# Attention and two feed-forward layers on one core: the order of attention's work from a greedy model in the kernel, and one ring of PSUM tiles for scores and maxima

## The chip, the cores and the metric

The kernel runs on one core of a Trainium2 chip. The metric is device time in microseconds (us), lower is better. Times are those of single executions, and the median of several runs stands for the kernel.

## The reference

Attention with a mask from hashing, over 2 batches of 8 heads (16 heads in all, 768 tokens, 64 dimensions), and then two feed-forward layers over 1536 tokens of 512 features (2048 inside). All data are fp32. Cut to what is computed:

```python
q_bits = (einsum('bhsd,dk->bhsk', q, proj) > 0)      # 6 bits, k_bits likewise
mask = q_bucket[:, :, :, None] == k_bucket[:, :, None, :]
scores = where(mask, scale * q @ k.T, -1e9)
scores = scores - max(scores, axis=-1)
attn = exp(scores)
attn = attn / (sum(attn, axis=-1) + 1e-09)
x = (attn @ v)  # heads side by side: (1536, 512)
h = x @ moe_w_in;   x = maximum(0.01 * h, h) @ moe_w_out
h = x @ moe2_w_in;  out = (h * cos(h)) @ moe2_w_out
```

## The kernel before, in words

Matmuls run in a reduced fp32 format (`F32R`), so each operand is split into a high part (a cast) and a low part (the value minus its cast), and a product takes three matmuls: high by high, high by low, low by high.

`attention` (L91) works head by head; each head has 768 = 6 x 128 keys, and 768 queries that are two halves of 384 columns (`HS`). Four buffers `AT` (L661) hold the split q and k of a head, its hash bits, and the row of the maxima. Per head n:

- `load_qk` (L125) loads the raw q and k, `prep_hi` (L143) casts them on VectorE and copies parts of the cast to other partitions by DMA, `prep_lo` (L149) subtracts on GpSimd, with one more copy by DMA.
- `bits_mm` and `bits_wr` (L197, L206), once per half: three matmuls with the hash directions, a comparison on VectorE, and two more copies by DMA after the second half. A differing bit lowers a score by a huge amount, and so masks it.
- `max_mm` and `max_red` (L218, L224), 12 of each: approximate scores of 128 queries by 384 keys in a one-bank PSUM tile `sm`, and their maximum on VectorE. `max_fin` (L231) joins the two halves, takes the maximum with a floor (for a query without any partner) and writes a 0/1 flag, in two small VectorE instructions on SBUF tiles. `max_row` (L238) turns both into rows by one matmul, ScalarE copies them out of PSUM, and DMAs put the maxima into `AT` and the flag into `E`, a tile of 2 rows.
- per 128 keys k: `qk` (L253, four matmuls into a two-bank tile `st`), `exp_a` and `exp_b` (L262, L273), `p_lo` (L282), `pv` (L296, four matmuls for part 0, two for part 1, into `pv`). A letter per k in `MODE` and `MODES` says how the exponential is split: A takes it twice on ScalarE, once rounded and once in place in PSUM, and subtracts on VectorE; B takes it once into `pf`, casts on ScalarE and subtracts on GpSimd; C casts on VectorE and subtracts on GpSimd; D casts and subtracts on VectorE.
- `pv_e` (L290) starts the accumulation with the sum of all v for queries that have no partner. `evac` (L310) copies the result and the sum of the exponentials out of PSUM. `recip` (L318) adds 1e-9, inverts, and spreads the inverse over 64 partitions by way of DRAM. `xmul`, `xhi`, `xlo` (L330 to L345) scale the result and split it into `XH` and `XL`, the input of the feed-forward layers.
- once in four heads: `load_v`, `v_hi`, `v_lo`, and `sum_v` with `sum_vr`, the sums of v over the tokens.

PSUM has eight banks: two `st` tiles of two banks, two `sm` tiles of one bank (maxima, bits, rows, sums), one `pv` tile of two. Each engine runs its instructions in the order in which the program issues them, and so does SyncE (SP) with its DMAs. The order is by sorted positions: `at` (L427) gives each step a number, head times 6 plus an offset from the table `K` (L37), and L473 issues the steps in the order of these numbers. Head 0 has its own code (`first`, `first_rest`, `max_whole`).

During heads 12 to 15 the first four chunks of feed-forward weights are prepared (`CHUNK_START`, `STAGE`, `Weights.stages` L490): they arrive as raw 64-bit words, and per chunk take two ScalarE, four VectorE and one GpSimd instruction of 128x1024. They use the memory of V and of the `AT` buffers as these come free. Then `moe` (L552) runs the two layers; it and the weights' code are the same before and after.

Of the kernel before, what the change touches and what calls it, by code (L numbers as in the profile page):

```python
# [30 lines left out]
MODE = "DBABBA"  # L31
MODES = {12: 'DBABBB', 13: 'BBABAA', 14: 'BBBBDA', 15: 'CDDDAA'}
ENG = dict(ph="V", pl="G", vh="G", vl="G", ev="A", xm="G", xh="V", xl="G")
CHUNK_START = (76.75, 83.91, 86.56, 96.03)
SHIFT = {2: 2.094}
STAGE = (0, 1.29, 1.88, 4.24, 4.46)
K = dict(  # L37
    ea=[0.01, 0.01, 0.01, 0.01, 0.01, 0.01],
    eb=[0.266, 0.025, 0.267, 0.02, 0.764, 0.862],
    lo=[0.733, 0.198, 0.93, 0.274, 0.938, 0.974],  # L40
    p0=[2.403, 2.19, 2.388, 2.41, 2.303, 1.7],
    p1=[2.578, 2.609, 2.72, 2.752, 2.806, 1.913],
    pe=2.084,
    ev=0.056,
    rec=10.899,
    xm=13.1,
    xh=16.761,
    xl=17.769,
    mx=[[0.364, 0.414], [0.085, 0.485], [0.328, 0.485], [0.328, 0.691], [0.237, 0.41], [0.523, 0.195]],
    rd=0.01,  # L50
    mf=-4.444,
    mr=-3.391,
    bm=[-12.668, -12.522],
    bw=0.01,
    ph=-15.546,
    pl=-15.374,
    ld=-24.393,
    vld=-30.087,
    vh=[-25.855, -12.685],
    vl=[-20.717, -11.738],  # L60
    sv=-2.83,
    svr=0.01,
    sv0=0.842,
    m1=[-5.464, -3.992, -1.927, -5.01, -3.499, -2.802],
    mf1=-1.615,
    mr1=-1.132,
)
GLV = 8
# [14 lines left out]
def f32(ap):  # L83
    return ap.bitcast(F32)
# [6 lines left out]
def attention(tc, XH, XL, AT, VH, VL, qkt, v, proj, cst, heads=NH, feed=()):  # L91
    nc = tc.nc
    T, V, A, G, Q = nc.tensor, nc.vector, nc.scalar, nc.gpsimd, nc.sync
    with ExitStack() as ctx:
# [39 lines left out]
        raw[0] = raw_p.tile([128, S], F32, name="raw")  # L134
        for h in range(2):
            Q.dma_start(raw[0][:, h * HS:(h + 1) * HS], qkt[0, 0][:, h * HS:(h + 1) * HS])
        Q.dma_start(cs, cst)
        thr, wgt = cs[64:BM, 128:129], cs[64:BM, 129:130]

        E = [con.tile([2, S], F32R, name=f"e{i}") for i in range(2)]  # L140
        SV = [con.tile([2, 4, 128], F32R, name=f"sv{i}") for i in range(2)]

        def prep_hi(n):  # L143
            at = AT[n % NR]
            copy(ENG["ph"], at[:, 0], raw[n])
            Q.dma_start(f32(at[0:64, 2]), f32(at[64:128, 0]))
            Q.dma_start(f32(at[0:64, 3]), f32(at[64:128, 0]))

        def prep_lo(n):  # L149
            at = AT[n % NR]  # L150
            eng(ENG["pl"]).tensor_tensor(at[:, 1], raw.pop(n), f32(at[:, 0]), op=ALU.subtract)
            Q.dma_start(f32(at[64:128, 3]), f32(at[64:128, 1]))

        vraw = {}

        def load_v(g):
            t = vraw_p.tile([128, C, 4, 64], F32, name="vraw")
            Q.dma_start(t, v[g // 2, :, :, (g % 2) * 4:(g % 2) * 4 + 4, :])
            vraw[g] = t

        def vsl(g, pr):
            return (t[g % 2][:, :, pr, 0:3:2, :] for t in (VH, VL))

        def v_hi(g, pr):
            copy(ENG["vh"], next(vsl(g, pr)), vraw[g][:, :, 2 * pr:2 * pr + 2, :])

        def v_lo(g, pr):
            hi, lo = vsl(g, pr)
            eng(ENG["vl"]).tensor_tensor(lo, vraw[g][:, :, 2 * pr:2 * pr + 2, :], f32(hi), op=ALU.subtract)

        svp = {}

        def sum_v(g):
            ps = sm_ps.tile([2, 2, 2, 64], F32, name="sm")
            vs = (VH[g % 2], VL[g % 2])
            for c in range(C):
                for j in range(2):
                    T.matmul(ps, ones2, vs[j][:, c, :, 0:3:2, :], start=(c == 0 and j == 0), stop=(c == C - 1 and j == 1))
            svp[g] = ps

        def sum_vr(g):
            ps = svp.pop(g)
            h2 = sv_p.tile([2, 4, 64], F32R, name="svh")
            l2 = sv_p.tile([2, 4, 64], F32, name="svl")
            psf = ps.rearrange("p a b d -> p (a b) d")
            V.tensor_copy(h2, psf)
            V.tensor_tensor(l2, psf, f32(h2), op=ALU.subtract)
            V.tensor_scalar(l2, l2, cs[0:2, 1:2], None, op0=ALU.mult)
            for par in range(2):
                dst = SV[g % 2].rearrange("p (a b) d -> p a b d", b=2)[:, :, par, par * 64:par * 64 + 64]  # L190
                src = h2.rearrange("p (a b) d -> p a b d", b=2)[:, :, par, :]
                sl = l2.rearrange("p (a b) d -> p a b d", b=2)[:, :, par, :]
                V.scalar_tensor_tensor(dst, f32(src), cs[0:2, 0:1], sl, op0=ALU.mult, op1=ALU.add)

        bps = {}

        def bits_mm(n, h):  # L197
            at = AT[n % NR]
            cols = slice(h * HS, (h + 1) * HS)
            ps = sm_ps.tile([128, HS], F32, name="sm")  # L200
            T.matmul(ps[0:BM], PB[0], at[:, 0, cols], start=True, stop=False)
            T.matmul(ps[0:BM], PB[1], at[:, 0, cols], start=False, stop=False)
            T.matmul(ps[0:BM], PB[0], at[:, 1, cols], start=False, stop=True)
            bps[n, h] = ps

        def bits_wr(n, h, spread=True):  # L206
            at = AT[n % NR]
            cols = slice(h * HS, (h + 1) * HS)
            V.tensor_scalar(at[64:BM, 0, cols], bps.pop((n, h))[64:BM], thr, wgt, op0=ALU.is_ge, op1=ALU.mult)
            if h == 1 and spread:  # L210
                Q.dma_start(f32(at[64:R76, 2]), f32(at[96:BM, 0]))
                Q.dma_start(f32(at[64:128, 1]), f32(at[0:64, 0]))

        mxt = {}

        mps = {}

        def max_mm(n, t, h):  # L218
            at = AT[n % NR]
            ps = sm_ps.tile([128, HS], F32, name="sm")  # L220
            T.matmul(ps, at[0:R76, 0, t * 128:(t + 1) * 128], at[0:R76, 2, h * HS:(h + 1) * HS], start=True, stop=True)  # L221
            mps[n, t, h] = ps

        def max_red(n, t, h):  # L224
            if (t, h) == (0, 0):
                mxt[n] = sm_p.tile([128, 2, C], F32, name="mx")
            V.reduce_max(mxt[n][:, h, t:t + 1], mps.pop((n, t, h)), axis=AX.X)  # L227

        met = {}

        def max_fin(n):  # L231
            mx = mxt.pop(n)
            me = sm_p.tile([128, 2, C], F32R, name="me")
            V.scalar_tensor_tensor(me[:, 0], mx[:, 0], -HALF_BIG, mx[:, 1 if n else 0], op0=ALU.max, op1=ALU.max)
            V.tensor_scalar(me[:, 1], f32(me[:, 0]), -HALF_BIG, None, op0=ALU.is_le)
            met[n] = me

        def max_row(n):  # L238
            me = met.pop(n)
# [8 lines left out]
        pt = {}

        def mode(n, k):  # L250
            return MODES.get(n, MODE)[k]

        def qk(n, k):  # L253
            at = AT[n % NR]
            ps = st_ps.tile([128, 2, 512], F32, name="st")
            for h in range(2):
                o = ps[:, h, 0:HS]
                T.matmul(o, at[0:R76 + 1, 2, k * 128:(k + 1) * 128], at[0:R76 + 1, 0, h * HS:(h + 1) * HS], start=True, stop=False)  # L258
                T.matmul(o, at[:, 3, k * 128:(k + 1) * 128], at[:, 1, h * HS:(h + 1) * HS], start=False, stop=True)  # L259
            pt[n, k] = [ps, None, None, None]  # L260
# [463 lines left out]
```

## Time and profile before

| | us |
|---|---|
| median of 3 runs | 836.24 |
| lowest, highest | 833.68, 840.98 |
| the profiled execution, its own time | 835.71 |
| its span, first to last instruction | 833.9 |
| TensorE busy in the span | 790.7 (95%) |
| VectorE busy | 554.1 (66%) |
| ScalarE busy | 404.7 (49%) |
| GpSimd busy | 421.1 (51%) |

Times in rows count from the start of the span. PE is TensorE, PEld its weight loads, DVE VectorE, ACT ScalarE, POOL GpSimd, SP SyncE. The last three numbers of a row of stretches are TensorE's granted clock (1.00 is 2.4 GHz), the DMA engines' busy share and GB/s. `L286` is line 286 of the kernel. The instruction that ends a wait is named behind an arrow. A matmul's row is longer than its share of TensorE, since matmuls overlap.

### The profile page before, as it was taken

How to read it: one execution, taken by the hardware profiler on the slowest of the kernel's cores; microseconds unless marked ns; L12 is line 12 of the kernel's file. 1: busy time of each engine (PE TensorE's matmuls, PEld its weight loads, DVE VectorE, ACT ScalarE, POOL GpSimd, SP SyncE). 2: the span in 40 equal slices, each digit the busy share in tenths (PEclk: the TensorE clock that was granted, in tenths of full speed). 3: DMA queues.
4: the chain of work that ended last, by engine and by line, in shares of the span. 5: the costliest groups of instructions: out<-in, count | busy, mean ns of one | idle time of the engine just before them, and what ended most of it. 6: DMA issues, size and time to landing. Idle time of an engine off the chain costs nothing. (4 is left out here: it accounts for less than half of the span.)

```text
span 833.9 us, 9909 instructions
## 1 busy us (share of the span) xinstructions
PE 790.7 (95%) x3648; PEld 669.9 (80%) x3648; DVE 554.1 (66%) x770; ACT 404.7 (49%) x592; POOL 421.1 (51%) x253
## 2 busy tenths in 40 slices
PE   5799899998997799999999999999899999999998
PEld 3688798898887777888888888888688888888886
DVE  6878888989988888654456536636736656753333
ACT  3355476565576454434234323454755645644442
POOL 4645578578677643336425515665623532542221
PEclk9999999999999899999999999999999999999999
DMA  4523434433351124212202202201211210000012
GB/s 127 156 59 89 110 89 98 120 97 88 79 172 61 39 99 196 101 66 105 83 0 102 101 1 101 101 1 57 95 51 51 101 51 0 1 1 1 0 51 101
DMA packets 24024, 62.60 MB, mean 75 GB/s; under 512 B 7636, under 2 KB 11380, under 8 KB 19880
## 3 DMA queue, kind: packets, MB, share of 16 engines
q1 hardware_dynamic: 23976, 61.97, 24.1%
q8 instruction: 29, 0.48, 0.2%
q14 instruction: 19, 0.16, 0.1%
HBM read 46.21 MB, written 3.19 MB: 59 GB/s over the span
## 5 line engine op out<-in xcount | busy, mean ns | idle before, releaser
L605 POOL TENSOR_TENSOR gl<-gf,gh 128x512 fp32r<-128x512 f32 x88 | 130.4, 1482 | 272.8 <-ACT gh L604 216.9
L618 PE MATMUL y<-gh,at 128*128 128x512 f32 x576 | 178.6, 391 | 1.9 <-ACT ys L624 1.8
L576 PE MATMUL h<-XH,at 128*128 128x512 f32 x576 | 142.8, 390 | 1.6 <-POOL XH L118 1.6
L618 PEld LDWEIGHTS y<-gh,at 128*128 128x128 f32 x576 | 108.4, 189 | 25.5 <-ACT ys L624 2.2
L576 PEld LDWEIGHTS h<-XH,at 128*128 128x128 f32 x576 | 108.3, 188 | 24.6 <-POOL XH L118 2.0
L618 PE MATMUL y<-gl,at 128*128 128x512 f32 x288 | 112.9, 392 | 0.7 <-POOL gl L605 0.7
L227 DVE TENSOR_REDUCE mx<-sm 128x1 f32<-128x384 f32 x180 | 95.7, 549 | 20.9 <-PE sm L221 19.2
L286 POOL TENSOR_TENSOR pl<-pf,ph 128x768 fp32r<-128x768 f32 x48 | 90.9, 1896 | 35.1 <-ACT ph L278 18.8
L585 DVE TENSOR_TENSOR gf<-h,gf 128x512 f32<-128x512 f32 x48 | 33.0, 690 | 104.9 <-ACT gf L584 104.8
L584 ACT ACTIVATE gf<-h 128x512 f32<-128x512 f32 x48 | 28.6, 597 | 150.5 <-PE h L576 137.0
L271 ACT ACTIVATE pf<-st 128x768 f32<-128x768 f32 x65 | 52.7, 811 | 67.9 <-PE st L259 56.4
L590 DVE SCALAR_TENSOR_TENSOR gf<-ki,h 128x512 f32<-128x512 int32 x48 | 32.9, 686 | 73.9 <-ACT ki L589 73.9
L589 ACT ACTIVATE ki<-h 128x512 int32<-128x512 f32 x48 | 28.6, 597 | 103.8 <-PE h L576 103.8
L576 PE MATMUL h<-XL,at 128*128 128x512 f32 x288 | 77.2, 389 | 0.1
L512 POOL TENSOR_TENSOR at<-wsc,at 128x1024 fp32r<-128x1024 f32 x24 | 61.2, 2549 | 19.2 <-ACT at L515 16.0
L221 PE MATMUL sm<-at 76*128 76x384 f32 x180 | 62.4, 364 | 8.1 <-DVE mx L227 6.7
L258 PE MATMUL st<-at 77*128 77x384 f32 x192 | 68.5, 357 | 0.9 <-PE pv L303 0.6
L259 PE MATMUL st<-at 128*128 128x384 f32 x192 | 67.2, 350 | 0.0
L618 PEld LDWEIGHTS y<-gl,at 128*128 128x128 f32 x288 | 54.3, 189 | 12.4 <-POOL gl L605 1.1
L598 DVE SCALAR_TENSOR_TENSOR gf<-gf,h 128x512 f32<-128x512 f32 x48 | 32.9, 685 | 46.2 <-ACT gf L597 46.2
L576 PEld LDWEIGHTS h<-XL,at 128*128 128x128 f32 x288 | 54.1, 188 | 11.7 <-POOL XL L345 0.6
L604 ACT ACTIVATE gh<-gf 128x512 fp32r<-128x512 f32 x96 | 59.9, 624 | 3.2 <-DVE gf L585 2.5
(102 smaller groups left out, 1531.5 us busy)
## 6 DMA issues: line engine op xcount, KB each, us to landing
wrvh<-in_w_dram SPq DMA_DIRECT2D x16, 1024.0 KB
wrvl<-in_w_dram SPq DMA_DIRECT2D x16, 1024.0 KB
at<-at SPq DMA_DIRECT2D x60, 192.0 KB
raw<-in_qk_dram SPq DMA_DIRECT2D x15, 384.0 KB
vraw<-in_v_dram SPq DMA_DIRECT2D x4, 768.0 KB
rr<-dr SPq DMA_DIRECT2D x16, 192.0 KB
out_dram<-ys SPq DMA_DIRECT2D x12, 256.0 KB
at<-at SPq DMA_DIRECT2D x15, 36.0 KB
```

The source lines that it names most:

```text
L221: T.matmul(ps, at[0:R76, 0, t * 128:(t + 1) * 128], at[0:R76, 2, h * HS:(h + 1) * HS], start=True, stop=True)
L227: V.reduce_max(mxt[n][:, h, t:t + 1], mps.pop((n, t, h)), axis=AX.X)
L258: T.matmul(o, at[0:R76 + 1, 2, k * 128:(k + 1) * 128], at[0:R76 + 1, 0, h * HS:(h + 1) * HS], start=True, stop=False)
L259: T.matmul(o, at[:, 3, k * 128:(k + 1) * 128], at[:, 1, h * HS:(h + 1) * HS], start=False, stop=True)
L271: A.activation(p[3], p[0][:, :, 0:HS], AF.Exp, scale=SCALE)
L286: e.tensor_tensor(halves(p[2]), p[3], halves(f32(p[1])), op=ALU.subtract)
L512: G.tensor_tensor(lf, sc, f32(hf), op=ALU.subtract)
L576: T.matmul(ps, w[:, 0, k], x[:, k, cols], start=(j == 0), stop=(j == 3 * KT - 1))
L585: V.tensor_tensor(g, ps, g, op=ALU.max)
L604: A.activation(gh, g, AF.Copy)
L605: (V if s < GLV else G).tensor_tensor(gl, g, f32(gh), op=ALU.subtract)
L618: T.matmul(y, w[:, 1, e], x, start=(j == 0 and i == 0), stop=(j == GRP - 1 and i == 2))
```

## The change

It rewrites `attention`; `moe`, `Weights` and `Feed` stay. Part by part:

1. *Order.* The table `K` and the sort are gone. Each step is added to a `Plan` with its engine, its kind, a cost from the table `COST`, a key, the steps that it needs, and the ring of buffers that it takes and gives back. `Plan.order` runs a greedy model of five in-order queues: the step that can start first is issued next, and among those of one engine that can start equally early the one with the lowest key. DMAs have a cost for SP, then a shared wire and a latency. What it returns is the order in which the program issues.
2. *PSUM.* Three `st` tiles of two banks in place of two `st` and two `sm`. Scores, maxima, bits, rows and sums take them in turn.
3. *Maxima.* One two-bank tile and one reduction over 768 keys per 128 queries, six per head. The floor and the flag are taken by VectorE from the transposed row in PSUM, not before it; ScalarE's copy of the row is gone.
4. *Casts.* Those of raw q and k, V, the exponentials and XH are all on ScalarE (before: VectorE, some GpSimd).
5. *Low parts.* `LO` says per head and k who subtracts: V takes the exponential twice on ScalarE and subtracts from PSUM on VectorE, G goes by `pf` and GpSimd. 60 of 96 are G (48 were on GpSimd before); in most heads 4 of 6.
6. *Sums.* `E` and `SV` are tiles of 128 partitions with zeros in most rows; the constant 1e-9 is added by rows of theirs in the `pv_e` matmul, and `recip` is a lone reciprocal. The split of the sums of v takes two small ScalarE steps and one VectorE step.
7. *Head 0* goes through the same code, except its first casts; three copies within `AT[0]` are DMAs instead of ScalarE copies. The zeros of `E` and `SV` and the constants of V are written by GpSimd at the start.

```diff
-MODE = "DBABBA"
-MODES = {12: 'DBABBB', 13: 'BBABAA', 14: 'BBBBDA', 15: 'CDDDAA'}
+LO = [{0: 'GGGVVV', 1: 'VGVGGG', 12: 'VGGGGG', 14: 'GGVVVV', 15: 'VGVVGV'}.get(n, "VGGGVG") for n in range(NH)]
...
+COST = dict(
+    load=0.5, hi=0.83, d2=0.55, d3=0.55, lo=1.87, dl=0.55, bm=1.06, bw=1.1, db2=0.7, db1=0.55,
+    mm=0.351, mr=0.953, rt=0.12, fl=0.4, dr=0.75, de=1.3, neg=0.65, qk=0.702, ex=0.83, cv=0.83, subV=0.95, subG=1.87,
+    pe=0.351, pv=0.702, pw=0.351, ev=0.83, lc=0.55, rc=0.18, dw=0.45, rr=0.55, xm=2.2, xh=0.83, xl=1.87,
...
+class Plan:
...
+        while len(done) < len(self.items):
+            best = None
+            for e in "PVAGQ":
+                if ready[e]:
+                    ts = [(start(it), it) for it in ready[e]]
+                    first = min(t for t, _ in ts)
+                    t, it = min(((t, it) for t, it in ts if t <= first + 1e-9), key=lambda x: x[1]["key"])
+                    if best is None or t < best[0]:
+                        best = (t, it)
...
-        st_ps = pool("st", 2, space=bass.MemoryType.PSUM)
-        sm_ps = pool("smp", 2, space=bass.MemoryType.PSUM)
+        st_ps = pool("st", 3, space=bass.MemoryType.PSUM)
...
-            copy(ENG["ph"], at[:, 0], raw[n])
+            A.activation(AT[n % NR][:, 0], raw[n], AF.Copy)
...
+        def max_mm(n, t):
...
+            ps = st_ps.tile([128, 2, 512], F32, name="st")
             for h in range(2):
+                T.matmul(ps[:, h, 0:HS], at[0:R76, 0, t * 128:(t + 1) * 128], at[0:R76, 2, COL[h]], start=True, stop=True)
...
+            V.reduce_max(mx[n][:, t:t + 1], mps.pop((n, t))[:, :, 0:HS], axis=AX.XY)
...
-            V.scalar_tensor_tensor(me[:, 0], mx[:, 0], -HALF_BIG, mx[:, 1 if n else 0], op0=ALU.max, op1=ALU.max)
-            V.tensor_scalar(me[:, 1], f32(me[:, 0]), -HALF_BIG, None, op0=ALU.is_le)
...
+            T.matmul(rps[n][0:C, 0, 0:128], mx.pop(n), ident, start=True, stop=True)
...
+            V.tensor_scalar(mts[n][:, 0], ps, -HALF_BIG, None, op0=ALU.max)
+            V.tensor_scalar(mts[n][:, 1], ps, -HALF_BIG, None, op0=ALU.is_le)
...
+            if LO[n][k] == "V":
+                pf[n, k] = sps.pop((n, k))
+                A.activation(pf[n, k], pf[n, k], AF.Exp, scale=SCALE)
+            else:
+                phi[n, k] = phi_p.tile([128, S], F32R, name="ph")
+                A.activation(halves(phi[n, k]), pf[n, k], AF.Copy)
...
+            (V if LO[n][k] == "V" else G).tensor_tensor(halves(plo[n, k]), pf.pop((n, k)), halves(f32(phi[n, k])), op=ALU.subtract)
...
-            V.tensor_scalar(rc, lcs.pop(n), 1e-9, None, op0=ALU.add)
-            V.reciprocal(rc, rc)
+            V.reciprocal(rcs[n], lcs.pop(n))
...
+                do("load", n, "Q", load_qk, n, take="raw" if n > 1 else None, after=[("load", n - 1), ("dr", n - 3)])
+                do("hi", n, "A", hi, n, after=[("load", n)] + old)
...
+                do("mm", n, "P", max_mm, n, t, k=t, j=(t,), take="st", after=[("db2", n), ("kb0", 0), ("kb0", 1), ("d2", n)])
+                do("mr", n, "V", max_red, n, t, k=t, j=(t,), after=[("mm", n, t)], take="mx" if t == 0 else None, give=[("mm", n, t)])
...
+                do("qk", n, "P", qk, n, k, k=k, j=(k,), take="st",
+                   after=[("dr", n), ("neg", n), ("d3", n), ("dl", n), ("db1", n), ("db2", n)])
...
-        for w in sorted(work, key=lambda w: w[:2]):
-            w[2](*w[3])
+        for it in plan.order():
+            it["fn"]()
```

## Rows read from the trace of the kernel before

**Rows 1.** Stretches: length, busy us of PE, PEld, DVE, ACT, POOL; clock; DMA
```profile
0.00:49.09 49.09, 35.53 (x136) 27.24 (x137) 36.06 (x66) 16.88 (x24) 23.72 (x29) 0.97 0.47 125
49.09:104.43 55.34, 50.73 (x261) 45.47 (x260) 47.00 (x80) 29.06 (x39) 31.78 (x19) 0.94 0.36 93
104.43:232.25 127.82, 121.94 (x674) 112.80 (x673) 113.85 (x199) 77.83 (x104) 93.30 (x52) 1.00 0.39 96
232.25:300.47 68.22, 57.11 (x281) 51.65 (x280) 60.48 (x76) 43.02 (x56) 47.25 (x22) 0.92 0.30 99
300.00:834.00 534.00, 525.84 (x2306) 433.13 (x2305) 297.15 (x354) 237.90 (x371) 225.09 (x133) 1.00 0.17 60
120.00:135.00 15.00, 13.91 (x76) 12.57 (x75) 13.65 (x24) 8.73 (x12) 13.41 (x8) 1.00 0.31 75
```

**Rows 2.** Timeline of TensorE, steady part: start us, us, engine line op
```profile
110.36 0.34 PE L258 MATMUL st<-at 77*128 77x384 f32 x1
110.54 0.34 PE L259 MATMUL st<-at 128*128 128x384 f32 x1
...
112.47 0.34 PE L258 MATMUL st<-at 77*128 77x384 f32 x1
```

**Rows 3.** Timeline of ScalarE: `evac` of heads 0, 3, 4, 11 and 15
```profile
49.09 0.81 ACT L114 ACTIVATE os<-pv 128x768 f32<-128x768 f32 x1 [1.57 <-PE pv L303]
...
104.43 0.81 ACT L114 ACTIVATE os<-pv 128x768 f32<-128x768 f32 x1 [1.57 <-PE pv L303]
119.00 0.81 ACT L114 ACTIVATE os<-pv 128x768 f32<-128x768 f32 x1 [1.60 <-PE pv L303]
...
232.25 0.81 ACT L114 ACTIVATE os<-pv 128x768 f32<-128x768 f32 x1 [1.59 <-PE pv L303]
...
300.47 0.82 ACT L114 ACTIVATE os<-pv 128x768 f32<-128x768 f32 x1 [0.81 <-POOL XL L345]
```

**Rows 4.** Waits of TensorE, 49 to 300 us: total, times, longest
```profile
PE sm L221 <- DVE mx L227: 6.7, 6, 3.4
```

**Rows 5.** Timeline of TensorE, start: first matmul, first scores, and their pace
```profile
5.59 0.62 PE L201 MATMUL sm<-at,pb 128*108 128x384 f32 x1 [5.59 <-DVE pb L359]
...
19.38 0.66 PE L258 MATMUL st<-at 77*128 77x384 f32 x1 [0.30 <-DMA at<-mt]
...
20.16 0.52 PE L258 MATMUL st<-at 77*128 77x384 f32 x1
20.48 0.52 PE L259 MATMUL st<-at 128*128 128x384 f32 x1
```

**Rows 6.** Timeline of all engines, 268 to 278 us
```profile
269.66 4.29 DVE L234 SCALAR_TENSOR_TENSOR me<-mx 128x6 fp32r<-128x6 f32 x1
...
270.35 3.57 POOL L286 TENSOR_TENSOR pl<-pf,ph 128x768 fp32r<-128x768 f32 x2
...
274.21 0.28 PE L241 MATMUL sm<-ident,me 128*12 128x128 f32 x1 [4.03 <-DVE me L235]
```

**Rows 7.** Groups of VectorE: count, busy us, mean ns of one
```profile
L227 DVE TENSOR_REDUCE mx<-sm 128x1 f32<-128x384 f32 x180 | 95.7, 549 | 20.9 <-PE sm L221 19.2
...
L234 DVE SCALAR_TENSOR_TENSOR me<-mx 128x6 fp32r<-128x6 f32 x16 | 16.5, 1030 | 0.5
...
L280 DVE CAST ph<-pf 128x768 fp32r<-128x768 f32 x18 | 14.3, 795 | 2.9 <-ACT pf L271 2.9
...
L321 DVE TENSOR_SCALAR rc<-lc 128x6 f32<-128x6 f32 x16 | 11.6, 724 | 1.3 <-DMA lc<-os 1.3
```

**Rows 8.** Single lines: shortest, median, longest of one in ns
```profile
L379 DVE TENSOR_REDUCE mx<-st x6: 947/952/958, 10.4 to 15.4; 128x1 f32<-128x768 f32 x6
...
L286 POOL TENSOR_TENSOR pl<-pf,ph x48: 1791/1846/2678, 32.9 to 287.1; 128x768 fp32r<-128x768 f32 x48
...
L286 DVE TENSOR_TENSOR pl<-pf,ph x17: 918/947/2977, 23.4 to 296.3; 128x768 fp32r<-128x768 f32 x17
...
L278 ACT ACTIVATE ph<-pf x47: 828/845/857, 28.7 to 277.1; 128x768 fp32r<-128x768 f32 x47
```

More of the change, by code (lines that the diff above doesn't have):

```diff
@@ L88, in halves, with __init__, add, order @@
     return ap.rearrange("p (a b) -> p a b", a=2)
-def attention(tc, XH, XL, AT, VH, VL, qkt, v, proj, cst, heads=NH, feed=()):
+class Plan:
+    def __init__(self, rings, free):
+        self.rings, self.free = rings, dict(free)
+        self.items, self.index = [], {}
+    def add(self, name, e, kind, key, fn, after=(), take=None, give=(), cost=None):
+        deps = [self.index[d] for d in after if d is not None and d in self.index]
+        it = dict(name=name, e=e, kind=kind, key=(key, len(self.items)), fn=fn, deps=deps, take=take, give=list(give),
+                  cost=COST[kind] if cost is None else cost, out=[], left=len(deps))
+        for d in deps:
+            d["out"].append(it)
+        self.items.append(it)
+        self.index[name] = it
+    def order(self):
+        free = {e: self.free.get(e, 0.0) for e in "PVAGQ"}
+        ready = {e: [] for e in "PVAGQ"}
+        taken = {r: [] for r in self.rings}
+        wire = 0.0
+        for it in self.items:
+            if it["left"] == 0:
+                it["at"] = 0.0
+                ready[it["e"]].append(it)
+        done = []
+        def start(it):
+            t = max(free[it["e"]], it["at"])
+            r = it["take"]
+            if r is not None:
+                n = len(taken[r]) - self.rings[r]
+                if n >= 0:
+                    t = max(t, taken[r][n].get("end", 1e9))
+            return t
+        while len(done) < len(self.items):
[7 more added lines that the diff above has]
+                        best = (t, it)
+            t, it = best
+            e, c = it["e"], it["cost"]
+            assert t < 1e8, ("stuck", [(i["name"], i["take"]) for q in ready.values() for i in q])
+            if e == "P" and t < 25:
+                c *= 1.9
+            ready[e].remove(it)
+            it["start"], free[e] = t, t + c
+            end = t + c
+            if e == "Q":
+                wire = max(wire, end + 0.3) + KB[it["kind"]] / 190.0
+                end = wire + 0.8
+            it["fin"] = end
+            if it["take"] is not None:
+                it["slot"] = {}
+                taken[it["take"]].append(it["slot"])
+            for g in it["give"]:
+                self.index[g]["slot"]["end"] = end + 0.06
+            for o in it["out"]:
+                o["left"] -= 1
+                o["at"] = max(o.get("at", 0.0), end + LAT[o["e"]] * (o["e"] != e or e == "Q"))
+                if o["left"] == 0:
+                    ready[o["e"]].append(o)
+            done.append(it)
+        self.done = done
+        return done
@@ L92, in attention @@
+def attention(tc, XH, XL, AT, VH, VL, qkt, v, proj, cst, fd, more_raws, heads=NH):
     nc = tc.nc
@@ L154, in attention @@
[L154 to L227, printed above, removed]
@@ L248, in attention @@
[L248 to L260, printed above, removed]
@@ L344, in xlo @@
[L344 to L345 removed]
+        E = [con.tile([128, S], F32R, name=f"e{i}") for i in range(2)]
+        SV = [con.tile([128, 4, 128], F32R, name=f"sv{i}") for i in range(2)]
         PB = [con.tile([128, BM], F32R, name=f"pb{s}") for s in range(2)]
@@ new lines, in sum_v, with sv_parts @@
+        def sum_v(g):
+            ps = st_ps.tile([128, 2, 512], F32, name="st")
+            vs = (VH[g % 2], VL[g % 2])
+            for c in range(C):
+                for j in range(2):
+                    T.matmul(ps[0:65, 0, 0:256], ones, vs[j][:, c, :, 0:3:2, :], start=(c == 0 and j == 0), stop=(c == C - 1 and j == 1))
+            svp[g] = ps
+        def sv_parts(g):
+            ps = svp[g][:, 0, 0:256].rearrange("p (a b d) -> p a b d", a=2, b=2)
+            dst = SV[g % 2].rearrange("p (a b) (c d) -> p a (b c) d", b=2, d=64)[:, :, 0:4:3]
+            return ps, dst
```

503 lines of the change are left out of this document (257 added, 246 removed).

## The prediction

> **What bounds the kernel now.** I read three things in order: busy time by stretch, then the starts of single matmuls, then the waits. The execution has two stages. From 300 us on the two feed-forward layers keep TensorE busy for 525.84 of 534 us [rows 1]; the change leaves their code alone, so that stage is carried over as it is. Attention ends with the last head's `evac`, at 300.47 us [rows 3]. Its own bound is less plain. TensorE is busy 35.53 + 50.73 + 121.94 + 57.11 = 265 us there [rows 1], which looks nearly full, but busy time overstates: in an undisturbed run twelve matmuls of 384 columns start between 110.36 and 112.47, so one costs 2.11 / 12 = 0.176 us, although each row is 0.34 us long [rows 2]. Matmuls times 0.176 us is the work of a stretch (the 48 narrower ones of `sum_v` make this a little too high); what is left over is excess that a better order could take away:
>
> - up to 49.09, from the first matmul at 5.59: 43.5 - 136 x 0.176 = 19.6 us
> - 49.09 to 104.43: 55.3 - 261 x 0.176 = 9.4 us
> - 104.43 to 232.25: 127.8 - 674 x 0.176 = 9.2 us
> - 232.25 to 300.47: 68.2 - 281 x 0.176 = 18.7 us
>
> That is 57 us in all [rows 1, 2, 3, 5]. The Trainium skill (Perfetto Trace Analysis, Identifying the Most-Contended Engine) says that matmul busy time is a poor measure of the room left, since matmuls overlap. By busy time the room would be 294.9 - 265 = 30 us, and a perfect order would give 806; by starts it is 57 us. The trace agrees with the rule: 0.34 us rows start 0.176 us apart.
>
> Who causes the excess? Among the waits of TensorE the longest in total is for VectorE's maxima (L221 <- L227, 6.7 us) [rows 4], and the longest single one for their floor (L241 <- L235, 4.03 us) [rows 6]. VectorE is the second full engine, 113.85 of 127.82 us in the third stretch [rows 1]. It is also slow at bad times: `max_fin`'s 128x6 instruction, 1.03 us on average, takes 4.29 us at 269.66, while GpSimd's subtractions run, and ends with them at 273.9 [rows 6, 7].
>
> **The change, part by part** (per head; the third stretch holds eight heads).
>
> VectorE now: 113.85 / 8 = 14.2 us. (a) Twelve one-bank reductions of 0.549 become six two-bank ones. Their price is seen on head 0: 0.952 [rows 7, 8]. 6.59 - 5.71 = 0.9 us less. (b) The floor leaves VectorE's SBUF tiles: -1.03 us for L234; two small operations on the transposed PSUM row come instead. No row has them; I bound each by nothing and by 0.55 us (the 128x384 reduction, which reads far more from PSUM) and take the middle, 0.3. (c) Casts to ScalarE: 14.3 / 16 = 0.9 us for `exp_b`; those of raw and XH come on top and I leave them out. (d) The add before the reciprocal goes into TensorE's constant row: -11.6 / 16 = 0.7 us. (e) Two instead of three subtractions on VectorE, all from PSUM now: -0.95 us, and none of the 2.98 us cases. VectorE falls to 14.2 - 4.5 + 0.6, about 10.3 us of some 14.6: no longer the bound. The bits of a head become one two-bank operation, bounded by once and twice the 0.55 of L227's form, against two today: taken as no change.
>
> ScalarE now: 77.83 / 8 = 9.7 us. It gains a cast of `exp`, one of raw, half of one for XH and half of one for V, three times 0.845 [rows 8], and loses the copy of the row. About 12.2 us of 14.6, 84%. Today's idle time hides it; without that cover each cast would cost its 0.85 us.
>
> GpSimd now: 93.30 / 8 = 11.7 us. One more subtraction per head (60 of the 96 in all, 48 before) at 1.85 [rows 8] gives 13.5 us of 14.6, 92%. It is the tightest of the three helpers. Its new zero fills fall in the first 15 us, ahead of head 1's remainder, which no matmul awaits before the row of head 0 is out; their cost is between 0 and 3 us, taken as 0.
>
> TensorE: same matmuls, 80 of 384 columns per head. `pv_e` contracts 128 rows instead of 2; its two matmuls could cost between nothing more and as much again, 0.35 us, and I take nothing, since the matmuls of 77 and of 128 rows in rows 2 and 5 keep one pace.
>
> SyncE: twelve DMAs per head before and after. Head 0 gets three copies by DMA in place of ScalarE. `lc`, the write of the reciprocal and `rr` are now separate items which the planner puts in SP's order when it expects their input; behind a late one stand the loads and copies of a head that is at least one head away. Cost between 0 and 1 us a head, taken as 0.
>
> Three two-bank tiles take the place of two two-bank and two one-bank tiles. Scores, maxima, bits, rows and `sum_v` now take turns in one ring: a wait on the oldest tile holds the whole TensorE queue. That is the price side; see the second case.
>
> Now the excess again. *Start*: 5.59 to 19.38 is a chain of head 0 (bits, six maxima, row, DMA) that stays. It holds 25 matmuls, 4.4 us of work, so 9.4 of the 19.6 us stay. Matmuls 0.32 us apart stand there until about 28 us [rows 5], another 3 stay. Of the last 7 I take 4. *49 to 104*: VectorE's waits, 7 of 9.4. *104 to 232*: half of the heads already run at TensorE's pace, 14.57 us from 104.43 to 119.00 [rows 3]; 4 of 9.2. *232 to 300*: the stalls behind VectorE and the matmuls at the lower clock after them go (the granted clock is 0.92 over this stretch, a mean of 1.2 and 2.4 GHz [rows 1]), but the weight stages stay on VectorE and still meet GpSimd; 14 of 18.7. Sum 29 us. The new waits of ScalarE and GpSimd are in what I leave: 28 us, of which 12 are the start.
>
> 835.71 - 29 = 806.7, say **807 us**. The profiled execution is 0.5 us below the median of the runs; I make no correction. A measurement of this kernel tells about 1% from no change.
>
> **The rivals.**
>
> *The ring of three becomes the bound.* A head takes 14.25 tiles; with three slots and a mean hold h it lasts 4.75 h. A score tile subtracted on VectorE holds its slot through four matmuls, two exponentials and the subtraction, 0.7 + 0.81 + 0.81 + 0.95 (an exponential taken at the 0.81 of `evac`, also two banks) [rows 2, 3, 8], some 4.3 us with waits; one for GpSimd about 2.0; a maximum 0.35 + 0.95 and a wait, 1.8. Mean 2.2 us, 10.6 us a head: not the bound. With one more us of wait on each tile h is 3.3 and a head 15.7 us: 45.1 + 15 x 15.7 = 280.6, 20 us less than 300.47: 816 us. For it: ScalarE at 84%, in order. Against: the mean has room for half as much again.
>
> *GpSimd becomes the bound, slower.* Every GpSimd subtraction stands ahead of two matmuls. If GpSimd can only keep the share that it has now, 93.30 / 127.82 = 73%, a head lasts 13.5 / 0.73 = 18.5 us: 45.1 + 277 = 322.6, 22 us later: 858 us. The point that decides: below 13.5 / 17.0 = 79% attention is longer than now, below 77% the kernel is over 1% slower. Against: from 120 to 135 it was busy 13.41 of 15 us, 89% [rows 1], so it can. The Trainium skill (GPSIMD Engine Reference, Engine selection) advises VectorE for elementwise work, GpSimd being about twice as slow with two inputs; the trace agrees, 1846 against 947 ns [rows 8]. By that rule twelve more subtractions there are a mistake, and this is the outcome.
>
> *The order does not fit the chip.* The order is now built from a table of costs. If the chip strays from it (DMA landings above all), new waits eat the 29 us: 836, no change.
>
> **How the numbers follow.** Forecast 0.62, ring 0.20, no fit 0.08, GpSimd 0.10. If all but the start's 12 us goes, 57 - 12 = 45 us are won: 791. The upper end must take in the ring with some more wait: 828. Range 791 to 828. Faster by over 1% (below 828): 0.62 + 0.20 and a little of the third, less some of the second, 0.82; within 1%: 0.08; slower: 0.10.
>
> **What would show it.** Right: last `evac` near 271 us; VectorE's busy time in attention down by over 70 us, with no small operation above 1 us outside the weight stages; `evac` intervals of 14.6 to 15.2 us; the granted clock 1.00 in attention's last stretch; TensorE's waits now name ScalarE or GpSimd. Wrong: `evac` intervals above 16 us with TensorE waiting for GpSimd's subtraction (the third case) or scores and maxima waiting for a tile's release (the second), or a feed-forward stage longer than 534 us, which no term here has.

## The result, and the profile after

The changed kernel takes 814.58 us (median of 4 runs, 813.16 to 818.02) against 837.47 for the kernel before (833.68 to 840.98): ratio 0.9734 [0.9677, 0.979], faster by 2.7%. The sign and the range held; the centre, 807, was 8 us too low. The profiled execution has a span of 814.0 us, 19.9 less than before's 833.9. In run 10 below one of the four executions took 1302.19 us, at a granted clock of 0.56; its ratio leaves that one out.

The page of the kernel after, busy time per engine:

```profile
PE 780.3 (96%) x3648; PEld 669.6 (82%) x3648; DVE 472.0 (58%) x581; ACT 436.7 (54%) x630; POOL 438.0 (54%) x280
```

VectorE gave up 82 us, ScalarE took 32 and GpSimd 17: the work has moved to the two engines that had room. Where that paid is seen in the `evac` rows of ScalarE (L114 before, L388 now; start us, us), here of heads 3, 11, 12, 13 and 15:

```profile
89.25 0.79 ACT L388 ACTIVATE os<-pv 128x768 f32<-128x768 f32 x1
...
210.47 0.81 ACT L388 ACTIVATE os<-pv 128x768 f32<-128x768 f32 x1
...
224.93 0.81 ACT L388 ACTIVATE os<-pv 128x768 f32<-128x768 f32 x1 [0.33 <-PE pv L379]
...
250.88 0.81 ACT L388 ACTIVATE os<-pv 128x768 f32<-128x768 f32 x1 [2.78 <-PE pv L379]
...
275.39 0.81 ACT L388 ACTIVATE os<-pv 128x768 f32<-128x768 f32 x1
```

The last one comes 25 us earlier than in [rows 3]. Heads 4 to 11 take (210.47 - 89.25) / 8 = 15.2 us each (before 16.0), and head 13 alone takes 26.0. The stretches of after, cut at the same `evac`s as [rows 1], with head 13 and the feed-forward stage by themselves (length, busy us of PE, PEld, DVE, ACT, POOL; granted clock, DMA share, GB/s):

```profile
0.00:43.29 43.29, 31.23 (x136) 25.42 (x137) 28.83 (x45) 21.37 (x29) 29.07 (x51) 1.00 0.58 155
43.29:89.25 45.96, 45.75 (x264) 44.20 (x263) 29.76 (x39) 36.45 (x48) 36.35 (x20) 1.00 0.47 120
89.25:210.47 121.22, 120.77 (x673) 114.00 (x672) 75.35 (x98) 94.62 (x126) 102.33 (x57) 1.00 0.42 102
210.47:275.39 64.92, 55.79 (x278) 52.37 (x277) 45.80 (x48) 45.62 (x58) 42.33 (x20) 0.89 0.27 85
...
224.93:250.88 25.95, 19.06 (x83) 17.00 (x81) 22.36 (x20) 14.24 (x17) 20.64 (x9) 0.80 0.30 97
...
275.00:814.00 539.00, 527.11 (x2306) 434.02 (x2305) 292.70 (x353) 239.00 (x373) 227.87 (x133) 0.99 0.17 61
```

Matmuls times 0.176 us, taken from each length as in the prediction (the first stretch again from 5.59; the first matmul now starts at 6.30, so 0.7 of its 13.8 us lie ahead of it), leaves this excess of TensorE:

| stretch, by heads | before | forecast gain | after | gain |
|---|---|---|---|---|
| 0 | 19.6 | 4 | 13.8 | 5.8 |
| 1 to 3 | 9.4 | 7 | -0.5 | 9.9 |
| 4 to 11 | 9.2 | 4 | 2.8 | 6.4 |
| 12 to 15 | 18.7 | 14 | 16.0 | 2.7 |
| attention | 57 | 29 | 32.1 | 25 |
| feed-forward stage | | 0 | | -5 |

So heads 1 to 12 now run at TensorE's own pace, more than forecast, and two places fell short. In the last stretch 25.95 - 83 x 0.176 = 11.3 of the 16.0 us lie in head 13, and the granted clock there is 0.80, a mean of 1.2 and 2.4 GHz. And the first feed-forward matmul starts at 275.2 (before 300.2), so that stage lasts 538.8 us instead of 533.7. The waits of TensorE say who is late; first those from 43 to 275 us (total, times, longest):

```profile
PE pv L379 <- DVE pl L366: 5.8, 2, 4.1
PE st L344 <- DVE pl L366: 1.5, 1, 1.5
PE pv L379 <- POOL pl L366: 1.1, 2, 0.8
```

The 6.7 us for the maxima [rows 4] and the 4.03 us for the floor [rows 6] are gone, but for 0.3 us. What is left is mostly in head 13, 6.9 us in all, and the longest wait there is for a subtraction. In the timeline of VectorE and GpSimd before it, L565 to L574 are weight stages:

```profile
232.24 3.06 POOL L574 TENSOR_TENSOR at<-wsc,at 128x1024 fp32r<-128x1024 f32 x1
...
232.36 0.67 DVE L565 TENSOR_SCALAR wsc<-wsc 128x1024 f32<-128x1024 f32 x1
...
233.07 2.78 DVE L566 TENSOR_SCALAR wsc<-wsc 128x1024 int32<-128x1024 int32 x1
...
235.26 2.29 POOL L366 TENSOR_TENSOR pl<-pf,ph 128x768 fp32r<-128x768 f32 x1
...
235.88 2.75 DVE L569 SCALAR_TENSOR_TENSOR wsc<-wrvl,wsc 128x1024 int32<-128x1024 int32 x1
...
237.62 2.67 POOL L412 TENSOR_TENSOR xx<-os,rr 64x768 f32<-64x768 f32 x1
238.67 2.71 DVE L570 SCALAR_TENSOR_TENSOR wsc<-wrvl,wsc 128x1024 int32<-128x1024 int32 x1
241.30 0.94 DVE L366 TENSOR_TENSOR pl<-st,ph 128x768 fp32r<-128x768 f32 x1
```

Four weight instructions hold VectorE for 8.9 us, from 232.36 to 241.30; the planner has them at 1.45 + 2.5 = 3.95 (`w1` and `w2` in `COST`). The subtraction behind them, which two matmuls await, starts at 241.30. Read the ends: L566 ends at 235.85, 0.55 us after GpSimd's L574 (235.30); L366 on GpSimd, 1.85 us elsewhere, ends 1.70 us after L566; L569 ends 1.08 us after that, and so on in turn. Each lasts until the other engine's instruction has ended, and then for 0.12 to 0.14 us less than its shortest time elsewhere. After its wait for the subtraction TensorE's matmuls start 0.32 us apart for a while, not 0.176:

```profile
242.30 1.01 PE L379 MATMUL pv<-pl,vh 128*128 128x384 f32 x2 [4.08 <-DVE pl L366]
243.11 0.52 PE L344 MATMUL st<-at 77*128 77x384 f32 x1
243.43 0.52 PE L345 MATMUL st<-at 128*128 128x384 f32 x1
```

Some two dozen of them stand there until 250.2, which costs about 3.5 us. With the waits that is most of head 13's 11.3.

The second place is the start of the feed-forward stage. First TensorE's longest wait from 275 us on, then the timeline of the three helpers and TensorE:

```profile
PE y L680 <- ACT gh L666: 4.7, 1, 4.7
```

```profile
279.01 2.75 DVE L570 SCALAR_TENSOR_TENSOR wsc<-wrvl,wsc 128x1024 int32<-128x1024 int32 x1
281.68 0.18 DVE L397 RECIPROCAL rc<-lc 128x6 f32<-128x6 f32 x1
...
287.51 1.80 POOL L412 TENSOR_TENSOR xx<-os,rr 64x768 f32<-64x768 f32 x1 [2.21 <-DMA rr<-dr]
289.35 0.84 ACT L418 ACTIVATE XH<-xx 128x768 fp32r<-128x768 f32 x1 [6.49 <-POOL xx L412]
290.10 1.06 ACT L646 ACTIVATE gf<-h 128x512 f32<-128x512 f32 x2
...
292.11 1.22 PE L680 MATMUL y<-gh,at 128*128 128x512 f32 x2 [4.65 <-ACT gh L666]
```

The last head's cast into `XH` (L418) stands in ScalarE's queue ahead of the first feed-forward activation (L646). It needs the last head's reciprocal, which itself stands behind a weight stage, then two DMAs and a product on GpSimd. ScalarE waits 6.49 us for it, and the first `y` matmul 4.65 us for ScalarE. Before, `xhi` had this one cast on GpSimd (`ENG["xh"] if n < heads - 1 else "G"`), the engine that makes the product.

### The profile page after: what moved, and what is told of

Read it like the earlier page. It is cut to its first block, busy times and chain, and to the rows that moved or that the text cites. A ratio compares the mean times of both kernels' runs of the same rounds, so it can differ in the third digit from the quotient of the medians.

```text
span 814.0 us, 9866 instructions
## 1 busy us (share of the span) xinstructions
PE 780.3 (96%) x3648; PEld 669.6 (82%) x3648; DVE 472.0 (58%) x581; ACT 436.7 (54%) x630; POOL 438.0 (54%) x280
## 5 line engine op out<-in xcount | busy, mean ns | idle before, releaser
L366 POOL TENSOR_TENSOR pl<-pf,ph 128x768 fp32r<-128x768 f32 x60 | 112.5, 1879 | 34.6 <-ACT ph L362 22.2
L273 DVE TENSOR_REDUCE mx<-st 128x1 fp32r<-128x768 f32 x96 | 91.0, 956 | 45.4 <-PE st L267 43.5
L646 ACT ACTIVATE gf<-h 128x512 f32<-128x512 f32 x48 | 28.5, 596 | 149.0 <-PE h L638 138.0
L574 POOL TENSOR_TENSOR at<-wsc,at 128x1024 fp32r<-128x1024 f32 x24 | 60.4, 2515 | 28.7 <-ACT at L577 28.7
L680 PEld LDWEIGHTS y<-gl,at 128*128 128x128 f32 x288 | 54.6, 189 | 12.8 <-POOL gl L667 1.1
L638 PEld LDWEIGHTS h<-XL,at 128*128 128x128 f32 x288 | 54.1, 188 | 11.3
L354 ACT ACTIVATE pf<-st 128x768 f32<-128x768 f32 x60 | 48.4, 807 | 20.4 <-PE st L345 18.4
L680 PE MATMUL y<-gh,wx 128*128 128x512 f32 x192 | 59.1, 389 | 0.0
```

The source lines that it names most:

```text
L273: V.reduce_max(mx[n][:, t:t + 1], mps.pop((n, t))[:, :, 0:HS], axis=AX.XY)
L354: A.activation(pf[n, k], sps.pop((n, k)), AF.Exp, scale=SCALE)
L366: (V if LO[n][k] == "V" else G).tensor_tensor(halves(plo[n, k]), pf.pop((n, k)), halves(f32(phi[n, k])), op=ALU.subtract)
L574: G.tensor_tensor(lf, sc, f32(hf), op=ALU.subtract)
L638: T.matmul(ps, w[:, 0, k], x[:, k, cols], start=(j == 0), stop=(j == 3 * KT - 1))
L680: T.matmul(y, w[:, 1, e], x, start=(j == 0 and i == 0), stop=(j == GRP - 1 and i == 2))
```

## The experiments

Runs 1 to 5 ask where the missing 8 us went; the others which part of the change brought the gain. Runs 4, 5, 10 and 11 are planned anew (another `LO`, `COST` or ring) with the keys that stood for the old ones, which counts against them. "Less" and "more" are against after's 814.58 us where nothing else is said. The runs were taken in three sets (1, 2, 6 and 7; 3, 4, 5 and 8; 9 to 12), beside which the kernel before took 838.57, 836.45 and 835.35 us (837.47 beside after), so a difference of some 2 us across sets is no finding.

**Run 1: the last head's cast on GpSimd, behind its own product, as before the change.**

```diff
-            A.activation(xsl(n, XH), xt[n // 2], AF.Copy)
+            if n == heads - 1:
+                G.tensor_scalar(xsl(n, XH), xt[n // 2], 1.0, 1.0, op0=ALU.mult, op1=ALU.mult)
+            else:
+                A.activation(xsl(n, XH), xt[n // 2], AF.Copy)
...
-                do("xh", n, "A", xhi, n, after=[("xm", n)])
+                do("xh", n, "G" if n == heads - 1 else "A", xhi, n, after=[("xm", n)], cost=1.15 if n == heads - 1 else None)
```

> The kernel after, with the last head's cast of XH given to GpSimd (as before the change) instead of ScalarE. Theory: that cast stood on ScalarE ahead of the first feed-forward instruction and waited 6.5 us for the last inverse, so TensorE lost 4.65 us waiting for gh and 0.9 us more, partly at the lower clock; without it the wait for gh goes and the time falls by 4 to 7 us, to about 809 us (ratio to before 0.967). Rival: the first feed-forward matmuls are held by the fourth weight chunk, late in any case; then under 1.5 us comes back and a wait for GpSimd's weight subtraction stands in its place.

Measured: 807.97 us, ratio 0.9635 [0.9618, 0.9653], 6.6 less than after. The wait for `gh` is gone, and the stage from the first `h` matmul (275.1) to the end is 532.2 us long. The whole loss of the feed-forward stage was this one instruction.

**Run 2: each weight stage from its own chunk.** `Feed.stage(c, j)` ran the next step of the oldest open chunk, whatever `c` was. The new plan overlaps two chunks, so steps ran at other places than planned.

```diff
-            self.busy.append(self.W.stages(c))
+            self.of = getattr(self, "of", {})
+            self.of[c] = self.W.stages(c)
+            self.busy.append(self.of[c])
...
-        self.busy[0 if j else -1].pop(0)()
+        self.of[c].pop(0)()
```

> The kernel after, with one fault of the feed mended: a weight stage that the plan issues for chunk c runs chunk c's next step, not the oldest open chunk's. Where the plan overlaps two chunks, steps ran in other places than planned. Theory: head 13's interval of 26 us is caused by this in part; mended, the interval falls to about 20 us and the time by 3 to 6 us. Rival: what costs is how long VectorE's four weight instructions take beside GpSimd (8.9 us for one chunk against 3.95 planned), in whatever place; then the time moves by less than 1.5 us either way.

Measured: 808.34 us, ratio 0.9639 [0.9614, 0.9665], 6.2 less. Head 13 falls from 26.0 to 21.6 us, head 14 from 15.0 to 13.0. The 4.7 us wait of run 1 is untouched, as it should be.

**Run 3: both.**

> The kernel after with both mends: the last head's cast of XH on GpSimd, and each weight stage running its own chunk's step. They act in different places (the first feed-forward steps, and heads 13 and 14), so the gains add up: 814.6 - 6.6 - 6.2, about 802 us. Rival: both only move the same wait for the fourth chunk; then it stays at 807 to 808.

Measured: 804.33 us (803.94 to 804.53), ratio 0.9604 [0.9557, 0.965]: the best version, faster than both kernels. The gains seem to overlap a little, 10.3 us against 6.6 + 6.2, but run 3 is of another set. Its head 13 and feed-forward stage, in the columns of the stretches above:

```profile
224.00:245.40 21.40, 18.54 (x83) 16.51 (x81) 18.12 (x20) 14.34 (x17) 15.96 (x8) 0.84 0.31 109
270.00:802.00 532.00, 524.17 (x2306) 431.99 (x2304) 292.42 (x353) 238.31 (x372) 229.34 (x134) 1.00 0.17 62
```

Head 13 still takes some 6 us more than the others. TensorE waits 2.8 us in it for VectorE, and from 227.99 to 233.43 its 17 matmuls start 0.32 us apart, 2.4 us more than at 0.176. Runs 4 and 5 try to get these.

**Run 4: run 3, and all six subtractions of head 13 on GpSimd** (`13: 'GGGGGG'` in `LO`), so that none stands behind a weight stage.

> Both mends, and in head 13 all six low parts on GpSimd, none on VectorE (planned anew). Head 13 lasted 21.6 us with the feed mended, and TensorE waited there for VectorE's subtraction behind the weight stages. Theory that this queue is what is left: head 13 falls by 3 to 5 us, about 798 us. Rival: GpSimd, which then has two more subtractions of 1.85 us beside the weights' own, becomes late instead; 800 to 806 us, with the waits now for GpSimd.

Measured: 809.08 us, ratio 0.9662 [0.9615, 0.9709], 4.8 more than run 3 on the same chip. Head 13 takes 17.6 us, but head 12 takes 17.8 and head 14 20.9, with 4.31 us of wait ahead of a row's matmul. It waits for a maximum that now stands behind the weight stages on VectorE: the delay moved to the next thing behind them. Head 13 is as the theory had it, but the time is above both numbers.

**Run 5: run 3, and true prices for the planner** (`w1=3.4, w2=5.4`).

> Both mends, and the two VectorE steps of a chunk at the cost that the trace shows beside GpSimd (3.4 and 5.4 us against 1.45 and 2.5) in the plan's table. Theory that the plan's wrong price makes head 13's waits: 3 to 6 us faster than with both mends alone. Rival: the keys were set for the old prices, and the work is the same; no gain, or slower by up to 10 us.

Measured: 806.66 us, ratio 0.9641 [0.9582, 0.97]: no gain over run 3, rather 2.3 more. Head 13 takes 17.9 us, but heads 14 and 15 take 16.7 and 15.8, and the three together 50.4 against 46.4 in run 3: again the delay moved.

**Run 6: the new instructions without the chosen order.** All keys are zero, so the model issues what can start first; `Feed.stage` as in run 2, and a head's first casts wait for all readers of their buffer.

```diff
-    load=-52, hi=11, d2=-55, d3=-21, lo=-50, dl=-19, bm=-14.04, bw=-40, db2=-3, db1=-26, mm=-9, mr=18, rt=-22,
...
+    load=0, hi=0, d2=0, d3=0, lo=0, dl=0, bm=0, bw=0, db2=0, db1=0, mm=0, mr=0, rt=0, fl=0, neg=0, dr=0, de=0,
...
+FIX = {}
```

> The same instructions on the same engines as after, but with every key and every fixed key zero (the chunks' positions stay, the feed mended as above, and an AT buffer waits for all its readers), so that only the order differs. Theory that lighter VectorE work is most of the gain: still faster than before, at most 10 us above after, 815 to 825 us. Rival that the order is most of it: 840 us or more, slower than before, with TensorE idle for several us per head.

Measured: 873.39 us, ratio 1.0413 [1.038, 1.0446], slower than before the change. The lighter VectorE brings nothing without an order that suits it. The reverse, the old instructions in an order from the model, was not run.

**Run 7: the floor back ahead of the row, same order.** Two VectorE instructions on 128x6 SBUF tiles, issued just before the row's matmul, and ScalarE copies the row.

```diff
+            V.scalar_tensor_tensor(me[:, 0], m, -HALF_BIG, m, op0=ALU.max, op1=ALU.max)
+            V.tensor_scalar(me[:, 1], f32(me[:, 0]), -HALF_BIG, None, op0=ALU.is_le)
...
-            V.tensor_scalar(mts[n][:, 0], ps, -HALF_BIG, None, op0=ALU.max)
-            V.tensor_scalar(mts[n][:, 1], ps, -HALF_BIG, None, op0=ALU.is_le)
+            A.activation(mts[n], ps, AF.Copy)
```

> The kernel after, same order, with only the floor of the maxima undone: two VectorE instructions on a 128x12 SBUF tile ahead of the row's matmul, and ScalarE's copy of the row. Theory: they meet GpSimd's subtractions as before (mean of the first above 0.5 us, single ones of 2 to 4 us), and TensorE waits for them in order; 2 to 8 us slower than after. Rival: VectorE now has slack and the row is early in the order; then within 1.5 us of after.

Measured: 839.5 us, ratio 1.0022 [0.9991, 1.0054]: the whole gain is lost, 25 us, more than either number. TensorE's wait for the floor from 45 to 320 us, and the groups of the two instructions in this run:

```profile
PE st L281 <- DVE me L279: 16.8, 10, 2.7
```

```profile
L279 DVE TENSOR_SCALAR me<-me 128x6 fp32r<-128x6 f32 x16 | 16.7, 1041 | 0.5
...
L278 DVE SCALAR_TENSOR_TENSOR me<-mx 128x6 fp32r<-128x6 f32 x16 | 8.2, 510 | 0.3
```

Their shortest times are 0.170 and 0.155 us, their longest 1.75 and 2.29. But the edit also gave the row's matmul no distance from the floor, so part of the loss is the placement.

**Run 8: the same with a lead.** The floor stands where the row's matmul stood; the matmul, the copy and the row's DMAs come six TensorE steps later.

```diff
+            row = steps.pop(i)
+            late = [j for j, it in enumerate(steps) if j >= i and it["e"] == "P"][5]
...
+            steps[i:late + 1] = [dict(name=("mf", n), e="V", fn=lambda n=n: max_fin(n))] + rest + [row] + held
```

> The floor undone as before, but with lead: VectorE's two small instructions stand where the row's matmul stood in the order, and that matmul (with its copy and DMAs) comes six TensorE steps later (about 3 us). The first version of this run gave the chip no lead, and TensorE waited 19 us in all for the floor, up to 2.7 us at a time. Theory that missing lead was most of that loss: the wait shrinks to under 6 us and the time is at most 7 us above after's 814.6. Rival that the instructions themselves are the loss, since they stand on VectorE until GpSimd's subtraction ends: still 15 us or more above after.

Measured: 831.14 us, ratio 0.993 [0.9898, 0.9961]. The wait for the floor falls to 1.6 us, so about 8 of the 25 us were the missing lead. The other 16.6 stay; heads 4 to 11 take (222.80 - 94.20) / 8 = 16.1 us each, not 15.2. TensorE's waits from 45 to 320 us show a part of it:

```profile
PE pv L388 <- DVE pl L375: 5.7, 2, 3.6
PE pv L388 <- POOL pl L375: 4.1, 4, 1.6
...
PE st L353 <- DMA at<-mt: 3.4, 2, 2.3
```

The waits for GpSimd's subtractions are up from 1.1 us, and those for the row's own DMA are new; the 5.7 us for VectorE's were 5.8 before this edit. What else makes up the 16.6 us is not shown. They come to 1 us a head, as much as the floor took of VectorE before (1.03 [rows 7]), although VectorE is no longer the bound. They hold the later row too, so they are an upper end for the instructions alone.

**Run 9: casts of raw and XH on VectorE, same order.**

```diff
-            A.activation(AT[n % NR][:, 0], raw[n], AF.Copy)
+            V.tensor_copy(AT[n % NR][:, 0], raw[n])
```

and the same for `xhi`.

> The kernel after, same order, with the casts of raw q and k (15) and of XH (8) back on VectorE. Theory: VectorE has room for 0.55 us more per cast, but these casts read and write SBUF and meet GpSimd's subtractions, and what stands behind them waits; 3 to 12 us slower than after's 814.6, less the 6 us at the start of the feed-forward layers, which ScalarE's last cast no longer holds. Rival: the casts cost nothing on either engine, since both have idle time; then about 808 us, the 6 us alone.

Measured: 818.51 us, ratio 0.9791 [0.9719, 0.9863], some 4 more than after, though the intervals overlap; the last `evac` comes at 280.7, 5.3 us later. Its VectorE groups:

```profile
L233 DVE CAST at<-raw 128x768 fp32r<-128x768 f32 x15 | 18.2, 1212 | 1.7 <-PE st L251 1.3 <-DMA raw<-in_qk_dram 0.3
L418 DVE CAST XH<-xx 128x768 fp32r<-128x768 f32 x8 | 9.7, 1208 | 6.6 <-POOL xx L412 6.6
```

On average they take 1.21 us, the shortest 0.55; ScalarE needs 0.83. The wait for the last cast sits on VectorE now, and the feed-forward stage is 536.4 us long, between run 1 and after.

**Run 10: three and three** (`LO = ["VGVGVG"]` for every head: 48 subtractions on GpSimd as before, planned anew).

> The kernel after with three low parts of six on GpSimd in every head and three on VectorE (48 and 48, as the counts before; planned anew with the same keys). If GpSimd at 92% were the bound, giving it less makes heads 1 to 11 shorter than their present 15.2 us: faster than 812. Theory: TensorE is the bound there and VectorE holds tiles longer, so no gain; 815 to 830 us, slower through tiles that VectorE's share keeps longer in the ring.

Measured: 826.08 us, ratio 0.9874 [0.9802, 0.9946], 11.5 more than after. Relieving GpSimd brings nothing here, so nothing speaks for GpSimd as the bound of the kernel after. How much of the 11.5 us is the old keys is not known.

**Run 11: a ring of two `st` tiles** (`pool("st", 2)`, planned anew, with run 6's two mends).

> The kernel after with two tiles in the ring in place of three (planned anew; the feed mended and an AT buffer waits for all its readers, as in the run without keys). By the prediction's mean hold of 2.2 us a tile, 14.25 tiles a head and two slots give 15.7 us a head at best against 15.2 now: if that mean is right, 815 to 835 us. Rival: the mean hold is nearer to 3 us, and two slots give 21 us a head; 880 us or more, and three slots are then themselves near the bound.

Measured: 874.4 us, ratio 1.0454 [1.0355, 1.0552]. Heads 1 to 12 take 18.7 us on average. So a tile is held at most 18.7 x 2 / 14.25 = 2.6 us there on average; with three tiles the same hold allows 12.5 us a head, under the 15.1 seen.

**Run 12: the kernel before, one more subtraction per head on GpSimd (heads 0 to 11), same order.**

```diff
-MODE = "DBABBA"
+MODE = "BBABBA"
```

> The kernel before, with one part of the change alone and its order kept: the first exponential of a head is cast on ScalarE and subtracted on GpSimd (in heads 0 to 11 and 13 where mode D stood; four of six on GpSimd, as after), which takes a cast of 0.80 us and a subtraction of 1.29 us per head off VectorE. Theory that VectorE's load is what bounds before: 4 to 12 us faster than before. Rival: without an order made for it the freed time is idle; within 3 us of before, or slower where a subtraction now comes 0.9 us later.

Measured: 854.37 us, ratio 1.022 [1.0152, 1.0288]: slower, where my theory had it faster. VectorE has less to do, but its floor takes longer:

```profile
L234 DVE SCALAR_TENSOR_TENSOR me<-mx 128x6 fp32r<-128x6 f32 x16 | 28.1, 1758 | 0.5
```

against 1.03 us in [rows 7]. TensorE's waits for the maxima (L241 <- L227 and L221 <- L227) go from 3.4 and 6.7 us to 11.2 and 8.3. So this part of the change is worth nothing in the old order: one more GpSimd subtraction per head does harm there.

## Why the prediction was right, and where it was not

**VectorE stops being the bound: right.** The groups of VectorE after, to be held against [rows 7, 8], and GpSimd's subtraction:

```profile
L273 DVE TENSOR_REDUCE mx<-st 128x1 fp32r<-128x768 f32 x96 | 91.0, 956 | 45.4 <-PE st L267 43.5
...
L366 DVE TENSOR_TENSOR pl<-st,ph 128x768 fp32r<-128x768 f32 x36 | 34.4, 957 | 17.2 <-ACT st L359 15.7 <-issue 1.0 <-POOL at L237 0.3
...
L282 DVE TENSOR_SCALAR mt<-st 6x128 f32<-6x128 f32 x16 | 4.4, 274 | 6.2 <-PE st L277 5.7 <-DMA lc<-os 0.4
L283 DVE TENSOR_SCALAR mt<-st 6x128 f32<-6x128 f32 x16 | 4.3, 269 | 0.0
L397 DVE RECIPROCAL rc<-lc 128x6 f32<-128x6 f32 x16 | 3.0, 187 | 7.9 <-DMA lc<-os 7.7
```

```profile
L366 POOL TENSOR_TENSOR pl<-pf,ph 128x768 fp32r<-128x768 f32 x60 | 112.5, 1879 | 34.6 <-ACT ph L362 22.2 <-DMA wrvh<-in_w_dram 2.9 <-PE st L345 2.5
```

The reduction costs 0.956 (0.952 taken), the floor's two operations 0.27 each (0.3 taken), the subtraction from PSUM 0.957, and none of the 36 takes over 0.960. Per head of the third stretch VectorE has 75.35 / 8 = 9.4 us (10.3 forecast), ScalarE 11.8 (12.2), GpSimd 12.8 (13.5). The bits, taken as no change, became 0.29 us cheaper per head: 1.085 once for 0.686 twice. Heads 4 to 11 take 15.2 us (14.6 to 15.2 forecast for a head), and VectorE's busy time in attention fell by 78 us (over 70 forecast).

**The gain in heads 1 to 11: mechanism right, size too small.** Forecast were 7 + 4 us, measured 9.9 + 6.4. I left waits of ScalarE and GpSimd in the rest; there were hardly any. Runs 6 and 12 show that the lighter instructions do not bring this without an order for them, and run 7 that the order does not bring it without the floor in PSUM. How much the order would bring with all the old instructions is open.

**"232 to 300: 14 of 18.7": the step that failed most.** It brought 2.7. The prediction said that the weight stages stay on VectorE and still meet GpSimd, and then priced that at next to nothing. In place of the old stalls came one in head 13: 8.9 us of weight stages ahead of a subtraction, with matmuls at the lower clock after it. The sign "granted clock 1.00 in attention's last stretch" was wrong: it is 0.89. Run 2 shows that 6.2 us of it come from steps that ran at other places than planned. The rest is waits behind VectorE and matmuls at the lower clock (run 3); how to get it stays open, since runs 4 and 5 only moved it.

**"The feed-forward layers carried over as it is": wrong by 5 us.** The change left their code alone, but not what stands ahead of it in ScalarE's queue. The last head's cast went from GpSimd to ScalarE. I priced the casts by ScalarE's idle time in steady heads and didn't ask what is queued behind the last one. The sign for it, a stage longer than 534 us, was named and came; runs 1 and 3 bring it to 532. The last `evac`, for which 271 was given, comes at 275.4.

**The start, and the edits costed at nothing: near.** The start gave 5.8 us for the 4 forecast. GpSimd's zero fills, taken as 0, probably cost 0.7: with fills beside them, the four VectorE steps ahead of the first matmul (L203) take 1.17 us from 4.99, where before (L359), with the last fill over at 4.81, they took 0.49 from 4.96. No run leaves the fills out. With 2.8 us of excess left in eight heads, `pv_e`'s more rows and SyncE's new order can't cost more than 0.35 us a head together.

**The sum.** 29 forecast; 25 in attention less 5 after it makes 20 in the profiled executions (23 by the medians). With both places mended (run 3) the kernel takes 804.33, close to the 806.7 of my sum, but by other terms: more from heads 1 to 11, less from the last four.

**The rivals.** *Ring of three:* the mean hold is at most 2.6 us in run 11, against the 2.2 estimated, and still short of binding; in after, TensorE's waits for a tile of the ring come to 2.3 us from 43 to 275. *GpSimd bound:* it was busy 102.33 / 121.22 = 84% over eight heads, more than the 79% from which it would have cost nothing, and less on it was slower in run 10, though with the old keys. *Order does not fit the chip:* true in one place, the weight stages, where the table's 3.95 us stood for 8.9 (but run 5, with dearer weight stages in the table, was no faster). The sign that waits now name ScalarE or GpSimd was wrong: the longest in attention still names VectorE, whose subtraction stands behind weight stages.

## What to carry to other kernels

When work moves to another engine, look at the last instruction that moves, not only at the engine's share: in an in-order queue it holds whatever the next stage has put behind it, here 6.6 us for one cast of 0.84. The program must run the steps that the planner placed (6.2 us here); dearer prices in the planner's table on top of that brought nothing (run 5). Small VectorE steps on SBUF tiles can be cheap alone and dear beside a busy GpSimd; taking them on data in PSUM made their time steady.

## What I had not expected of the hardware

VectorE instructions whose operands lie in SBUF can last until the GpSimd instruction beside them has ended, in sizes large and small: 128x6 from 0.155 to 2.29 us (run 7) and 4.29 [rows 6], the 128x1024 weight steps from 0.69 to 2.78 and from 1.22 to 2.75, casts from 0.55 to 2.23 (run 9). Not all do: the 16 reciprocals (L397), also 128x6 in SBUF, stay within 0.175 to 0.193 us, the one at 121.81 amid GpSimd subtractions that last from 120.55 to 126.04. GpSimd is held in turn: at 232.24 L574 takes 3.06 us with VectorE's L565 of 0.67 us beside it, and 2.36 at 242.60, beside reductions from PSUM. With an operand in PSUM nothing of the kind is seen: L282 and L283 stay within 0.238 to 0.281 us through all heads. I had seen such rows in the trace of before, and had not expected that two small instructions a head could cost up to 16.6 us in all (run 8) on an engine with room.

The Trainium skill (SBUF — State Buffer, Who interferes with whom) states this as a lock: a VectorE instruction in a two-port mode needs a port pair that it shares with GpSimd, and so does one with two inputs from SBUF beside a GpSimd instruction that reads SBUF; whichever issues first has the pair for the whole instruction, and the other is blocked. The trace agrees in the ends of the rows of head 13 above: L569 ends 1.08 us after GpSimd's L366, and GpSimd's L412 1.7 us after L569. Who was first the starts do not show: L574 starts 0.12 us ahead of L565 and ends 2.27 us after it. By that rule the price of a weight step in head 13 is its own time plus what is left of a GpSimd instruction, and the planner's 3.95 us can't hold there.
